# Causal weighted sums with key blocks at 0, 128, 256 and 384 instead of 0, 64, 192 and 320

## The chip, the cores and the metric

One Trainium2 chip, one of its cores. The metric is device time in microseconds (us), the median of several runs of the whole kernel; the profile is of one further execution.

## What is computed

Three layers follow each other on 4 batches of 448 positions: causal attention with 12 heads of 64, a gated feed-forward layer with a short convolution, and a layer of 4 experts, each a causal attention with a head of 64, of which each position takes the best two. Cut to what matters:

```python
def causal(q, k, v):                      # one head, 448 x 64
    scores = q @ k.T / 8, masked above the diagonal
    a = softmax(scores)
    return a @ v                          # the weighted sum

x   = causal(q, k, v)                     # 4 batches x 12 heads, fp32
h   = relu(x @ w_in)                      # 768 -> 1024
x   = (h * sigmoid(conv3(h))) @ w_out     # 1024 -> 768
out = sum over 2 of 4 experts of w_e * causal(x @ wq[e], x @ wk[e], x @ wv[e]) @ wo[e]
```

So there are 4 x 12 + 4 x 4 = 64 causal heads. The kernel takes them in pairs (`o` is 0 or 1 for the two heads): 24 pairs of the first layer and 8 of the experts, 32 in all.

## The kernel before

Queries stand in four blocks, `Q0` = 0, 64, 192, 320 with `QN` = 64, 128, 128, 128 rows; block `c` sees the first `Q0[c]+QN[c]` keys, that is 64, 192, 320 or 448. A pair passes these steps.

- **Scores** (`scores`, L619). For most pairs queries and keys are split in two parts each (`prepare`, L740), and three products per block are added; each head fills 64 of TensorE's 128 rows, and the two heads work side by side (L670). Pair 0 alone (`WHOLE_QK`, L40) skips the split: its keys are padded with zeros to 128 rows (`prepare_whole`, L757), and L661 multiplies whole fp32 numbers, one head after the other.
- **Weights.** VectorE masks and takes the maximum (L647), ScalarE the exponential (L651), and VectorE, ScalarE or GpSimd divide by the sum (L692, L695). They lie in a tile `e`, queries on the partitions.
- **Turning** (`weigh`, L706). TensorE turns 16 squares of 128x128 of `e` (`tr`, L704), so that keys lie on the partitions. In the first four squares the last 64 keys of head 0 lie beside the first 64 of head 1 (their keys are stored in opposite orders). Four copies take the turned squares from PSUM to SBUF, one of 448 columns (`n0`) and three of 512 (`ab`), on ScalarE (L606) or VectorE (L608).
- **The weighted sum.** The values of the pair lie in a tile `block`. L723 is one product over all 128 columns of TensorE, the first 64 keys of both heads, 448 queries. L729 holds six products of 64 columns each, for the key blocks at 64, 320 and 192 and both heads; here the two heads fill the left and the right half of the columns and work side by side. Each fp32 product is recorded as two instructions.

So TensorE works in three arrangements: the whole array (L704, L723, L877 and others), two halves of rows (L670), two halves of columns (L729).

All other matrix products are those of the feed-forward and projections (L877, L984). Two weight matrices are multiplied into one at the start (`fold`, L837).

No loop sets the order. Every step is entered in a `Plan` (L165) with its engines, an estimated cost and the buffers that it needs; a list scheduler then writes out the instructions of each engine in one fixed order, which the chip follows. A table of numbers (`SHIFTS`, L60) moves ranks in it. `FILLS` (L54) enters 30 products of zeros (L1079), which the plan places where TensorE has nothing else. All DMAs are issued in one queue, SP's.

Of the kernel before, what the change touches and what calls it, by code (L numbers as in the profile page):

```python
# [39 lines left out]
WHOLE_QK = range(1)  # L40


TILES = (((0, 1, 1), (0, 2, 1), (0, 3, 1), (0, 3, 3)), ((1, 1, 1), (1, 2, 1), (1, 3, 1), (1, 3, 3)), ((0, 2, 2), (0, 3, 2), (1, 2, 2), (1, 3, 2)))
SWITCH = 0.2
# [5 lines left out]
PAIRS, VALUES, UNITS, SLABS, EN, PO = 18, 6, 15, 3, 3, 1  # L50
QUOTA = {"xs": 7, "qks": 4, "y": 4, "vs": 3, "vs2": 2, "w1": 3, "wraw": 1, "ab": 4, "qw": 1, "kb": 1, "raw": 1}
# [34 lines left out]
def f32(ap):  # L86
    return ap.bitcast(F32)
# [73 lines left out]
class Op:  # L161
    __slots__ = ("n", "engines", "fn", "deps", "after", "bufs", "new", "rank", "wait", "ready", "start", "end", "engine", "m", "issue", "banks", "port")


class Plan:  # L165
# [25 lines left out]
    def op(self, engines, fn, r=(), w=(), after=(), hold=(), m=128, issue=0.45, port=""):  # L191
# [4 lines left out]
        o.m, o.issue = m, issue  # L196
# [145 lines left out]
    def schedule(self, rank):  # L342
# [20 lines left out]
        dge = dma = load = port = 0.0  # L363
        coming = {e: [] for e in names}
# [25 lines left out]
        while left:  # L390
# [19 lines left out]
            for e in names:  # L410
# [8 lines left out]
                while lists[e]:  # L419
# [9 lines left out]
                    if t > now + 1e-9:  # L429
                        heapq.heappush(events, t)  # L430
                    elif not o.new or room(o.new, now):
                        wait = max(now, load + o.m / 1200) - now if e == "T" else 0.0
                        found.append((item[0] + 500 * wait, len(found), item))
                        if wait <= 1e-9 or len(found) == 12:
                            break
# [19 lines left out]
                elif e == "T":  # L455

                    begin = max(now, load + o.m / 1200)
# [66 lines left out]
def attention_moe_moe(ctx: ExitStack, tc: tile.TileContext, qk, vv, w_in, cw, w_out, wqk, wvg, wo, out):  # L524
# [12 lines left out]
    mask = base.tile([128, 768], F32, name="mask")  # L537
# [3 lines left out]
                            base=0, pattern=[[-1, 128]], channel_multiplier=1)  # L541
    tri = base.tile([128, 4, 4], F32, name="tri")
# [21 lines left out]
    for t in blocks:  # L564
        for o in range(2):
            nc.gpsimd.memset(t[HALF[1 - o], 0, o], 0.0)
# [19 lines left out]
    for name, kind, quota in (  # L586
            ("xs", pairs, QUOTA["xs"]), ("g", pairs, 8), ("qks", pairs, QUOTA["qks"]), ("wx", pairs, 12),
            ("y", pairs, QUOTA["y"]), ("q2", pairs, 2), ("k2", pairs, 2),
            ("vs", bk, QUOTA["vs"]), ("gx", gxk, 1), ("vs2", bk, QUOTA["vs2"]), ("w1", slabs, QUOTA["w1"]), ("wraw", half, QUOTA["wraw"]), ("wt", half, 2), ("wxr", half, 2), ("raw", half, QUOTA["raw"]),
# [546 lines left out]
```

## Time and profile before

| | |
|---|---|
| Median of 3 runs | 540.93 us (540.92 to 541.36) |
| The profiled execution, its own time | 540.68 us |
| Its span in the profile, first to last instruction | 538.9 us |
| TensorE's granted clock over the span | 1.00, that is 2.4 GHz |
| Busy: PE, DVE, ACT, POOL | 530.6, 413.1, 331.7, 97.5 us |

PE is TensorE multiplying and PEld TensorE loading weights, DVE is VectorE, ACT ScalarE, POOL GpSimd. A matmul's length in the profile includes the time until its last result is out, so that lengths of neighbours overlap; what an instruction costs its successors is the distance from start to start.

### The profile page before, as it was taken

The numbers are of one execution on the slowest core, as the hardware profiler recorded it, in microseconds if no ns is written. First come the engines' busy times: TensorE is split into PE (matmuls) and PEld (weight loads), VectorE is DVE, ScalarE is ACT, GpSimd is POOL, SyncE is SP. The second block draws the span as 40 slices with busy tenths as digits, with TensorE's granted clock in tenths as the row PEclk, the third lists the DMA queues.
The fourth block names the chain that finished last, engine by engine and source line by source line (L and its number), as shares of the span: only waits on it lengthen the run. The fifth ranks groups of instructions, "written<-read, shape, count | busy, mean of one in ns | idle before, by whom it ended". The sixth has DMA issues, their size and how long they took to land.

```text
span 538.9 us, 10192 instructions
## 1 busy us (share of the span) xinstructions
PE 530.6 (98%) x3550; PEld 437.5 (81%) x3552; DVE 413.1 (77%) x1224; ACT 331.7 (62%) x947; POOL 97.5 (18%) x122
## 2 busy tenths in 40 slices
PE   8999999999999999999999999999999999999999
PEld 4768887678888887899887778998887778999886
DVE  5997869999995578794669988964877898855461
ACT  3973637668995456762557885752866668534442
POOL 3630102342343121200024210000232000000020
DMA  8785327656466002646002472671004405520042
GB/s 252 241 233 141 115 75 243 188 196 226 145 231 165 2 17 53 216 148 216 0 18 81 136 229 84 226 237 42 2 2 137 155 1 176 183 111 1 1 161 103
DMA packets 43411, 69.91 MB, mean 130 GB/s; under 512 B 8928, under 2 KB 37344, under 8 KB 43360
## 3 DMA queue, kind: packets, MB, share of 16 engines
q1 hardware_dynamic: 43360, 69.26, 40.7%
q8 instruction: 28, 0.46, 0.4%
q14 instruction: 23, 0.19, 0.1%
HBM read 55.87 MB, written 13.37 MB: 128 GB/s over the span
## 4 chain that ended last, share of the span: by engine, by line
PE 69%; DVE 3%; ACT 2%; DMA 1%; issue 0%; DVEq 0%; ACTq 0%
PE pf L877 41%; PE bank L704 8%; PE bank L670 7%; PE bank L729 6%; PE bank L723 4%; PE pf L984 1%; DVE work L906 1%; DMA work<-in_w_in 1%; PE bank L877 1%; ACT e L651 1%; PE pf L1079 1%; DVE work L914 0%; ACT e L692 0%; DVE work L798 0%; DVE work L800 0%; ACT pair L606 0%
## 5 line engine op out<-in xcount | busy, mean ns | idle before, releaser
L877 PE MATMUL pf<-pair,slab 128*128 128x448 f32 (+2 forms) x984 | 215.7, 367 | 1.6 <-DVE wqks L614 0.8
L877 PEld LDWEIGHTS pf<-pair,slab 128*128 128x128 f32 x984 | 171.8, 188 | 23.7 <-issue 6.1
L651 ACT ACTIVATE e<-e,stat 128x320 f32<-128x320 f32 (+3 forms) x256 | 126.8, 498 | 24.0 <-DVE stat L647 23.7
L647 DVE CUSTOM_DVE_ANT_0 e<-bank,mask 128x320 f32<-128x320 f32 (+3 forms) x256 | 92.7, 414 | 5.4 <-PE bank L670 4.9
L877 PE MATMUL pf<-pair,wqks 128*128 128x448 f32 x384 | 81.6, 369 | 0.5 <-ACT pair L606 0.5
L704 PE MATMUL bank<-ident,e 128*128 128x128 f32 x512 | 74.8, 276 | 2.7 <-DVE e L695 1.8
L877 PEld LDWEIGHTS pf<-pair,wqks 128*128 128x128 f32 x384 | 71.4, 188 | 7.1 <-ACT pair L606 0.9
L704 PEld LDWEIGHTS bank<-ident,e 128*128 128x128 f32 x512 | 59.3, 140 | 21.2 <-issue 7.6
L608 DVE COPY work<-bank 128x512 f32<-128x512 f32 (+1 forms) x63 | 40.6, 666 | 25.1 <-PE bank L704 22.1
L614 POOL TENSOR_TENSOR pair<-work,pair 128x448 fp32r<-128x448 f32 (+1 forms) x35 | 43.5, 1256 | 53.5 <-ACT pair L606 25.4
L606 ACT ACTIVATE work<-bank 128x512 f32<-128x512 f32 (+1 forms) x69 | 38.7, 579 | 22.9 <-PE bank L704 17.7
L670 PE MATMUL bank<-pair,pair 64*64 64x64 f32 (+3 forms) x560 | 51.8, 292 | 0.0
L906 DVE SCALAR_TENSOR_TENSOR work<-hp,cws,work 128x448 f32<-128x448 f32 x64 | 43.8, 696 | 7.0 <-ACT work L901 6.8
L729 PE MATMUL bank<-work,block 128*64 128x128 f32 (+2 forms) x384 | 48.5, 388 | 0.0
L651 ACT ACTIVATION_READ_ACCUMULATOR e<-e,stat 128x1 f32 (+1 forms) x256 | 48.3, 189 | 0.0
L670 PEld LDWEIGHTS bank<-pair,pair 64*128 64x128 f32 (+1 forms) x560 | 40.1, 173 | 3.6 <-issue 1.6
L729 PEld LDWEIGHTS bank<-work,block 128*64 128x64 f32 x384 | 22.5, 136 | 23.9 <-issue 21.1
L692 ACT ACTIVATE e<-e,stat 128x448 f32<-128x448 f32 (+3 forms) x88 | 39.0, 508 | 3.6 <-DVE stat L687 3.4
L877 PE MATMUL pf<-wvs,pair 128*128 128x260 f32 x288 | 37.7, 286 | 0.0
L614 DVE TENSOR_TENSOR pair<-pf,pair 128x448 fp32r<-128x448 f32 (+3 forms) x32 | 15.4, 500 | 28.7 <-ACT pair L606 28.4
L877 PEld LDWEIGHTS pf<-wvs,pair 128*128 128x128 f32 x288 | 35.3, 188 | 1.2 <-issue 0.6
L606 ACT ACTIVATE pair<-pf 128x448 fp32r<-128x448 f32 (+3 forms) x32 | 13.3, 443 | 37.0 <-PE pf L877 36.9
(98 smaller groups left out, 596.7 us busy)
## 6 DMA issues: line engine op xcount, KB each, us to landing
slab<-w_scratch SPq DMA_DIRECT2D x24, 768.0 KB, 4.3
work<-in_w_out SPq DMA_DIRECT2D x8, 768.0 KB, 5.1
work<-in_w_in SPq DMA_DIRECT2D x8, 768.0 KB, 5.6
w_scratch<-slab SPq DMA_DIRECT2D x8, 768.0 KB, 4.1
work<-in_qk SPq DMA_DIRECT2D x24, 224.0 KB, 4.0
out<-work SPq DMA_DIRECT2D x24, 224.0 KB, 2.0
block<-in_vv SPq DMA_DIRECT2D x24, 192.0 KB, 3.3
slab<-wo_scratch SPq DMA_DIRECT2D x6, 768.0 KB, 4.3
```

Of the source, the lines that this page charges most:

```text
L606: nc.scalar.activation(dst(), src(), AF.Copy)
L608: nc.vector.tensor_copy(dst(), src())
L614: return lambda e: engine(e).tensor_sub(dst(), src(), f32(h()))
L647: nc.vector.tensor_tensor_reduce(out=ec(o, c), in0=bank(o, c), in1=m, scale=-0.125, scalar=3.0e38, op0=OP.add, op1=OP.min, accum_out=st[ro ...
L651: nc.scalar.activation(ec(o, c), ec(o, c), AF.Exp, bias=st[rows, 0, o, c:c + 1], scale=-1.0, accum_out=st[rows, 1, o, c:c + 1])
L670: nc.tensor.matmul(bank(o, c), q(s)[own, Q0[c]:Q0[c] + QN[c]], k(t)[own, kc(o, c)], start=i == 0, stop=i == 2)
L692: nc.scalar.activation(ec(o, c), ec(o, c), AF.Copy, scale=st[:QN[c], 3, o, c:c + 1])
L704: P.op({"T": TURN}, lambda _: nc.tensor.transpose(dst(), src(), ident[:, :]), r=r, w=keys)
L723: P.op({"T": 4 * S / 2400}, lambda _: nc.tensor.matmul(ps[:, :S], v[:, 0].rearrange("p o d -> p (o d)"), n0[:, :S], start=True, stop=False ...
L729: nc.tensor.matmul(ps[own, Q0[k]:S], v[:, k, o], part(o), start=False, stop=k == 2)
L877: nc.tensor.matmul(out_ap(), a(), b(), start=first, stop=end), r=r, w=[(ps, 0)])
L906: return lambda _: nc.vector.scalar_tensor_tensor(cv[:, :S], hp[:, i:S + i], cws[:, fc, i:i + 1], cv[:, :S], op0=OP.mult, op1=OP.add)
```

## The change

Key blocks now begin at 0, 128, 256 and 384, so the blocks of keys have 448, 320, 192 and 64 columns of queries to serve (`KEYS`). All products of the weighted sum, the first included, have 64 columns per head and two heads side by side: eight in place of seven (L764). Half of the 128 keys of a block lie behind the first 64 queries that the block serves; that quarter of the triangle is not copied, its place holds zeros from the start.

The turned weights go to one buffer of their own, `z` (`ZN` = 1), in eight copies in place of four: four of 64 partitions x 128 columns, two of 128 x 512, two of 128 x 256. The products start when all eight are in. Before, `n0` and three `ab` were four separate buffers.

To suit, head 1's keys are now the ones stored backwards, in blocks of 64 (`keys`; 256-byte runs), the values of a pair come in four DMAs of 256-byte runs instead of three, the experts' values have one double tile instead of four quarters of a shared kind, and their copies are cut otherwise. `WHOLE_QK` covers pairs 0 and 1. The plan counts 0.094 us for each change of TensorE's arrangement and puts an operation that needs one behind others (`CHANGE`, `TURNING`). `SHIFTS` is another table.

```diff
-WHOLE_QK = range(1)
+WHOLE_QK = range(2)
+KEYS = ((0, 448), (448, 320), (768, 192), (960, 64))
+def spread(z, width, first, step, n):
+    lo = min(first, width - 2 * step)
+    return z[:, lo:lo + 2 * step].rearrange("p (b c) -> p b c", b=2)[:, :, first - lo:first - lo + n]
+CHANGE, TURNING = 0.094, 2.0
...
-                        found.append((item[0] + 500 * wait, len(found), item))
+                        other = e == "T" and o.mode != mode
+                        found.append((item[0] + 500 * wait + TURNING * other, len(found), item))
...
     def weigh(e, v, v_r, dst):
-        ps, n0 = P.buf("po"), P.buf("ab")
-        t = P.buf("ta")
+        ps, z, t = P.buf("po"), P.buf("z"), P.buf("ta")
...
-        P.op(psum_cost(S, "AV"), high(lambda: n0[:, :S], lambda t=t: t[:, :S]), r=[(t, c) for c in range(4)], w=[(n0, 0)])
+        for o, own in enumerate(HALF):
+            for i, (first, step, src, near) in enumerate(((0, 448, 64, 128), (768, 192, 320, 128))):
+                P.op(psum_cost(128, "AV"), high(lambda own=own, n=1024 * o + first, step=step: spread(z, 2048, n, step, 64)[own],
+                                                lambda own=own, t=t, src=src: spread(t, 512, src, near, 64)[own]),
+                     r=[(t, c) for c in range(4)], w=[(z, (o, i))])
...
-        P.op({"T": 4 * S / 2400}, lambda _: nc.tensor.matmul(ps[:, :S], v[:, 0].rearrange("p o d -> p (o d)"), n0[:, :S], start=True, stop=False),
-             r=[(n0, 0)] + v_r, w=[(ps, 0)])
...
         def rest(_):
-            for k, part in ((1, lambda o: ab[o][:, :384]), (3, lambda o: ab[o][:, 384:]), (2, lambda o: ab[2][:, 256 * o:256 * o + 256])):
+            for k, (n0, n) in enumerate(KEYS):
                 for o, own in enumerate(HALF):
-                    nc.tensor.matmul(ps[own, Q0[k]:S], v[:, k, o], part(o), start=False, stop=k == 2)
+                    nc.tensor.matmul(ps[own, S - n:S], v(k, o), z[:, 1024 * o + n0:1024 * o + n0 + n], start=k == 0, stop=k == 3)
...
+    def keys(p, o, dst, w):
+        if o:
+            P.op(dma_cost(114688, 256), load(lambda: blocks64(dst()), blocks64(qk[p, HALF[1], 1])[:, ::-1]), w=w)
+        else:
+            P.op(dma_cost(114688, 1792), load(dst, qk[p, HALF[0], 1]), w=w)
```

The order of instructions that the plan writes out moves with it. The first place is TensorE's queue at the last weighted sum of the program, before (`work` holds the turned weights, `block` the values, `pair` and `slab` are operands of the last projection):

```order
L877 MATMUL bank_151<-pair_121,slab_142 128x448
L877 MATMUL pf_144<-pair_121,slab_142 128x448
L723 MATMUL bank_149<-work_143,block_100 128x448
L729 MATMUL bank_149<-work_143,block_100 64x384 x2
L729 MATMUL bank_149<-work_143,block_100 64x128 x2
L729 MATMUL bank_149<-work_143,block_100 64x256 x2
L877 MATMUL pf_144<-pair_121,slab_141 128x448
```

and of the change:

```order
L916 MATMUL bank_155<-pair_131,slab_151 128x448
L916 MATMUL bank_158<-pair_131,slab_151 128x448
L764 MATMUL bank_160<-z_113,values_110 64x448 x2
L764 MATMUL bank_160<-z_113,values_110 64x320 x2
L764 MATMUL bank_160<-z_113,values_110 64x192 x2
L764 MATMUL bank_160<-z_113,values_110 64x64 x2
L916 MATMUL pf_154<-pair_131,slab_150 128x448
```

The product over the whole array is gone, and four pairs of products stand where there were three. In the same queue over the whole program the arrangement changes 118 times before and 107 times after.

The second place is ScalarE's queue around the copies of the last two weighted sums, before (`bank` is PSUM):

```order
L606 ACTIVATE work_143<-bank_149 128x448
L606 ACTIVATE pair_121<-bank_148 128x448
L606 ACTIVATE work_143<-bank_147 128x512
L606 ACTIVATE work_143<-bank_146 128x512
L606 ACTIVATE pair_124<-bank_149 128x448
```

and of the change:

```order
L633 ACTIVATE z_113<-bank_156 64x2x64 x4
L633 ACTIVATE z_113<-bank_155 128x2x256
L633 ACTIVATE z_113<-bank_157 128x2x128 x2
L633 ACTIVATE pair_145<-bank_160 128x448
```

The copies of one weighted sum are seven rows here (the eighth is on VectorE). In the whole program 128 copies become 256, of which ScalarE has 132 and VectorE 124.

The third place is TensorE's queue near the start, before, where four of the products of zeros (`mask` holds them) stand between whole scores and the first folded weights:

```order
L661 MATMUL bank_149<-work_143 64x64
L1079 LDWEIGHTS mask
L1079 MATMUL pf_144<-mask 128x512
L1079 LDWEIGHTS mask
L1079 MATMUL pf_145<-mask 128x512
L661 MATMUL bank_150<-work_143 64x64
L1079 LDWEIGHTS mask
L1079 MATMUL pf_144<-mask 128x512
L1079 LDWEIGHTS mask
L1079 MATMUL pf_145<-mask 128x512
L877 MATMUL pf_144<-pair_121,slab_140 128x512
```

and of the change, where 19 of them stand ahead of the first row:

```order
L1110 LDWEIGHTS mask
L1110 MATMUL pf_153<-mask 128x512
L688 MATMUL bank_155<-work_152 128x448
L688 MATMUL bank_156<-work_152 128x448
L688 MATMUL bank_157<-work_152 128x320
L688 MATMUL bank_158<-work_152 128x320
L731 MATMUL bank_159<-ident,work_152 128x128
```

Of the 30 products of zeros, 12 stood ahead of the first real product before and 19 do now; 11 stood behind the last real product of the program, and none does now.

## Rows read from the trace of the kernel before

**Rows 1.** The page, parts 1 and 4: busy time; the chain by engine.

```profile
PE 530.6 (98%) x3550; PEld 437.5 (81%) x3552; DVE 413.1 (77%) x1224; ACT 331.7 (62%) x947; POOL 97.5 (18%) x122
...
PE 69%; DVE 3%; ACT 2%; DMA 1%; issue 0%; DVEq 0%; ACTq 0%
```

**Rows 2.** Waits of PE: us in total, times, longest us.

```profile
PE bank L704 <- DVE e L695: 1.8, 2, 1.1
PE pf L585 <- DVE tri L543: 1.7, 1, 1.7
```

**Rows 3.** Stretches: length, busy us (instructions) of PE, PEld, DVE, ACT, POOL; clock.

```profile
0.00:40.00 40.00, 35.91 (x213) 24.68 (x214) 33.33 (x104) 26.29 (x75) 18.04 (x37) 1.00 0.83 243
...
81.00:150.00 69.00, 67.03 (x469) 52.35 (x465) 67.03 (x165) 54.87 (x150) 23.13 (x18) 1.00 0.64 202
...
320.00:500.00 180.00, 180.00 (x1193) 151.47 (x1191) 137.29 (x421) 108.83 (x313) 15.07 (x22) 1.00 0.32 103
```

**Rows 4.** Groups of PE instructions by shape.

```profile
L723 PE MATMUL bank<-work,block 128*128 128x448 f32 x64 | 30.0, 550 | 0.0
L729 PE MATMUL bank<-work,block 128*64 128x384 f32 x128 | 27.7, 512 | 0.0
...
L729 PE MATMUL bank<-work,block 128*64 128x256 f32 x128 | 19.2, 379 | 0.0
...
L729 PE MATMUL bank<-work,block 128*64 128x128 f32 x128 | 12.4, 273 | 0.0
```

**Rows 5.** Timeline of PE, 300 to 312 us: start, length, instruction.

```profile
301.57 0.91 PE L723 MATMUL bank<-work,block 128*128 128x448 f32 x2
302.41 0.24 PE L670 MATMUL bank<-pair 64*64 64x64 f32 x2
...
304.16 1.52 PE L729 MATMUL bank<-work,block 128*64 128x384 f32 x12
305.61 0.66 PE L704 MATMUL bank<-ident,e 128*128 128x128 f32 x4
...
309.05 0.92 PE L723 MATMUL bank<-work,block 128*128 128x448 f32 x2
```

**Rows 6.** Timeline of PE near the end.

```profile
520.98 0.92 PE L723 MATMUL bank<-work,block 128*128 128x448 f32 x2
521.73 0.82 PE L704 MATMUL bank<-ident,e 128*128 128x128 f32 x6
...
535.20 2.55 PE L1079 MATMUL pf<-mask 128*128 128x512 bf16 x10
```

**Rows 7.** Timeline of PEld, from 304.15 to 304.23 us.

```profile
304.16 0.20 PEld L729 LDWEIGHTS bank<-work,block 128*64 128x64 f32 x4 [0.19 <-issue]
```

**Rows 8.** Timeline of PE at the start.

```profile
5.94 2.75 PE L1079 MATMUL pf<-mask 128*128 128x512 bf16 x12
8.76 0.74 PE L704 MATMUL bank<-ident,work 128*128 128x128 f32 x5
```

**Rows 9.** Groups of ACT copies by shape.

```profile
L606 ACT ACTIVATE work<-bank 128x512 f32<-128x512 f32 x48 | 27.8, 594 | 7.5 <-PE bank L704 6.4 <-PE bank L723 0.5 <-issue 0.2
...
L606 ACT ACTIVATE work<-bank 128x448 f32<-128x448 f32 x21 | 11.3, 543 | 15.4 <-PE bank L704 11.4 <-PE bank L877 1.8 <-DMA out<-work 1.4
...
L606 ACT ACTIVATE block<-pf 128x128 f32<-128x128 f32 x11 | 2.7, 280 | 6.4 <-PE pf L877 6.4
...
L606 ACT ACTIVATE slab<-bank 128x256 fp32r<-128x256 f32 x4 | 1.5, 378 | 0.4 <-PE bank L704 0.4
```

**Rows 10.** DMA issues: KB each, us to landing.

```profile
block<-in_vv SPq DMA_DIRECT2D x24, 192.0 KB, 3.3
...
block<-in_vv SPq DMA_DIRECT2D x48, 16.0 KB, 2.9
```

**Rows 11.** Page, part 5: weight loads of L729.

```profile
L729 PEld LDWEIGHTS bank<-work,block 128*64 128x64 f32 x384 | 22.5, 136 | 23.9 <-issue 21.1
```

**Rows 12.** 81 to 150 us, L729 alone: length, PE, PEld.

```profile
81.00:150.00 69.00, 9.09 (x72) 4.22 (x72) 1.00 0.64 202
```

More of the change, by code (lines that the diff above doesn't have):

```diff
@@ L161 @@
 class Op:
-    __slots__ = ("n", "engines", "fn", "deps", "after", "bufs", "new", "rank", "wait", "ready", "start", "end", "engine", "m", "issue", "banks", "port")
+    __slots__ = ("n", "engines", "fn", "deps", "after", "bufs", "new", "rank", "wait", "ready", "start", "end", "engine", "m", "issue", "banks", "port", "mode")
 class Plan:
@@ L565, in attention_moe_moe @@
         for o in range(2):
-            nc.gpsimd.memset(t[HALF[1 - o], 0, o], 0.0)
+            nc.gpsimd.memset(t[HALF[1 - o], 3, o], 0.0)
+    both_values = tiles("values", 1, [128, 4, 2, 2, 64], F32)
+    for t in both_values:
+        for o in range(2):
+            nc.gpsimd.memset(t[HALF[1 - o], 3, :, o], 0.0)
+    turned_weights = tiles("z", ZN, [128, 2048], F32)
+    for t in turned_weights:
+        for o in range(2):
+            for n0, n in KEYS:
+                nc.gpsimd.memset(t[HALF[1 - o], o * 1024 + n0:o * 1024 + n0 + 64], 0.0)
     weights = tiles("e", EN, [128, 2048], F32)
@@ L645, in mx @@
             def mx(_):
-                m = mask[rows, 448 - w:448] if c and o else mask[rows, 320:320 + w]
+                m = mask[rows, 384:384 + w] if c and o else mask[rows, 448 - w:448] if c else mask[rows, 320:384]
                 nc.vector.tensor_tensor_reduce(out=ec(o, c), in0=bank(o, c), in1=m, scale=-0.125, scalar=3.0e38,
@@ L670, in mm @@
                             nc.tensor.matmul(bank(o, c), q(s)[own, Q0[c]:Q0[c] + QN[c]], k(t)[own, kc(o, c)], start=i == 0, stop=i == 2)
-            P.op({"T": 0.27 + sum(3 * max(product(Q0[c] + QN[c]), QN[c] / 1200) for c in ORDER)}, mm, r=r,
-                 w=[(sbs[o][c], c) for c in ORDER for o in range(2)], hold=[e])
+            P.op({"T": 0.08 + sum(3 * max(product(Q0[c] + QN[c]), QN[c] / 1200) for c in ORDER)}, mm, r=r,
+                 w=[(sbs[o][c], c) for c in ORDER for o in range(2)], hold=[e], mode=1)
             for c in ORDER:
@@ L933, in load_cw, with halves @@
         single(lambda: raw[:, :6 * NF], 3 * NF, lambda: bits(cws).rearrange("p a b -> p (a b)"), [(raw, 0)], [(CWS, 0)])
-    def turn(step, o, dst, src, *more):
-        parts = [(lambda ap: ap, lambda ap: ap)] if o else turned
-        steps = [step(lambda d=d: d(dst()), lambda q=q: q(src()), *[lambda d=d, m=m: d(m()) for m in more]) for d, q in parts]
-        def fn(e):
-            for f in steps:
-                f(e)
-        return fn
+    def halves(step, o, own, ap, *more):
+        d = blocks64 if o else lambda ap: ap
+        q = (lambda ap: blocks64(ap)[:, ::-1]) if o else d
+        return step(lambda: d(ap()), *[lambda m=m, f=f: f(m()) for m, f in zip(more, (q, d))])
     def project(b, gs, gx):
@@ L1003, in project @@
-            P.op(cost[1], high(lambda n=n, c=c: lg[:n, b, c], lambda src=src: src()[:, 256:260]), r=[key], w=[(LG, (b, c))])
+                P.op(psum_cost(128, "AV"), high(lambda k=k: v[:, k, :, 0], lambda ps=ps: heads(ps, 0)), r=[(ps, 0)], w=[(v, (k, 0))])
+                for i in range(2):
+                    P.op(psum_cost(128, "AV"), high(lambda k=k, i=i: v[HALF[i], k, :, 1], lambda ps=ps, i=i: heads(ps, 1)[HALF[1 - i]]), r=[(ps, 0)], w=[(v, (k, 1 + i))])
+                for i in range(2):
+                    dst = (HALF[1 - i] if k or i else own), k + i
+                    P.op(psum_cost(4), high(lambda dst=dst: lg[dst[0], b, dst[1]], lambda ps=ps, i=i: ps[HALF[i], 256:260]), r=[(ps, 0)], w=[(LG, (b, dst[1], i))])
@@ new lines, in project @@
+                continue
+            for f in range(NF):
+                for m, s in ((128, 0), (64, 1))[::1 if f + 1 < NF else -1]:
+                    P.op({"T": product(260)}, lambda _, f=f, m=m, s=s, ps=ps: nc.tensor.matmul(
+                        ps[:m, :260], gx[:, f * 128:f * 128 + m], wvs[:, s, f], start=f == 0 and s == 0, stop=f + 1 == NF and s == 0),
+                         r=[(gx, f), (WV, (f, s))], w=[(ps, 0)], m=m)
+            xc = P.buf("xc")
+            P.op(psum_cost(260), high(lambda xc=xc: xc[own, :260], lambda ps=ps: ps[oth, :260]), r=[(ps, 0)], w=[(xc, 0)])
@@ new lines, in project @@
+            P.op({"V": on_vector(260)}, lambda _, ps=ps, xc=xc: nc.vector.tensor_add(xc[own, :260], ps[own, :260], xc[own, :260]),
+                 r=[(ps, 0)], w=[(xc, 0)])
+            for o in range(2):
+                P.op(copy_cost(128, "AV"), high(lambda o=o: v[HALF[o], 3, :, o], lambda xc=xc, o=o: heads(xc, o)[own]), r=[(xc, 0)], w=[(v, (3, o))])
+            P.op(copy_cost(4, "AVG"), high(lambda: lg[oth, b, 3], lambda xc=xc: xc[own, 256:260]), r=[(xc, 0)], w=[(LG, (b, 3, 0))])
+        vs = [(lambda k, o, a=a: v[:, k, a, o], [(v, (k, i)) for k in range(4) for i in range(3 if k < 3 else 2)]) for a in range(2)]
```

123 lines of the change are left out of this document (53 added, 70 removed), and 24 rows, old and new, of the table SHIFTS.

## The prediction

> **What bounds the kernel now.** I read the busy times first, then the chain that ended last, then TensorE's waits, then stretches of the span, and at last the instructions one by one. PE is busy for 530.6 of 538.9 us, and the chain runs through PE for 69% of the span where DVE has 3% and ACT 2% [rows 1]. The longest wait of PE by one cause adds up to 1.8 us, the next is the 1.7 us before the very first instruction [rows 2]. From 320 to 500 us PE has no idle time at all, with DVE at 137 and ACT at 109 of 180 us; only in the first 40 us does it stand idle for some 4 us [rows 3]. So the sum of what TensorE does sets the end, and an instruction that it no longer executes is gained in full, as long as the plan keeps finding it other work. The one stretch where another engine is as full is 81 to 150 us: DVE 67.0 and ACT 54.9 of 69 us [rows 3].
>
> **The change, part by part.**
>
> *The products.* One weighted sum costs now: L723, 0.75 us from its start to that of a transpose behind it [rows 6], and L729, 1.45 us from 304.16 to 305.61 [rows 5]. When L723 is followed by products in halves of rows instead of a transpose the distance is 0.84 us [rows 5], so a change of arrangement costs 0.09 us, and L729 without the change behind it 1.36. Together 2.11 us. What a column costs comes from the groups by shape: the 128 groups of 256 columns take 19.2 us and those of 128 take 12.4, that is 6.8 us for 32 sums x 128 columns, 1.66 ns per column of queries and pair of heads, four passes included [rows 4]. At this price 448 columns cost 0.74 us, what L723 costs too: the same time for a block with half the rows in use, or rather for two heads with 64 keys each. Afterwards the pair of heads has 448+320+192+64 = 1024 columns in halves where L729 had 768: 1.36 + 256 x 1.66 ns = 1.79 us. The gain is 2.11 - 1.79 = 0.32 us, for 32 sums -10.4 us. The uncertain part is the 64-column products, which the trace does not hold in this form: if loading their weights bounds them they cost what 128 columns cost, 0.11 us more, and the gain is 7.0 us. Four weight loads of L729 lie within 0.20 us [rows 7] and one takes 0.136 us on average [rows 11], so all four began within some 0.06 us of each other: the loads of the two halves overlap. I take -10.4, bounds -7.0 and -10.4.
>
> The Trainium skill, page "TensorE: Matmul & The Clock Gate", section "LDWEIGHTS (loading the stationary operand)", gives a load the number of its columns divided by 1.2 in ns; from that page, an estimate, four loads of 64 columns one after another take 0.21 us, as much as the products of 128 columns, and by it the sum would be 3.4 us smaller. The trace does not agree that the four stand one after another, and the same skill, page "TensorEngine Tiling (Array Packing)", section "Key Properties", lets separate tiles load in parallel.
>
> *Changes of arrangement.* The order has 107 instead of 118. 11 x 0.09 = -1.0 us; between -1.0 and 0, should the dearer ones be those that stay.
>
> *Pair 1 whole.* Its scores take 2 x 1024 columns at 1.66 ns, 3.40 us, in place of one L670 group, 1.75 us from 302.41 to 304.16 [rows 5]: +1.7. Nothing is split for this pair, which takes a copy and two subtractions off ACT, DVE and POOL in the first 40 us. If PE would have waited there anyway, the cost is 0. I take +1.7.
>
> *Products of zeros.* Twelve take 2.75 us, 0.23 each [rows 8]. Before, 11 of 30 stand behind the last product, at 535.20 [rows 6], where they delay nothing; afterwards all 30 stand ahead of it: +2.5 us. They stand where the plan finds nothing else to do, so they may take the place of the idle time in the first 40 us; then the cost is 0. PE's first real work, now at 8.76 us [rows 8], comes seven such products later, 1.6 us. I take +2.5, as an instruction in the queue is executed whether data came early or not.
>
> *The copies.* Before, one copy of 448 columns and three of 512, on ACT 0.54 + 3 x 0.59 = 2.33 us; afterwards four of 128 (nearest row 0.28, of twice the partitions), two of 512 and two of 256 (0.38): 1.12 + 1.19 + 0.76 = 3.07 us [rows 9]. That is +0.74 us per sum, 24 us over the run, spread over ACT and DVE, which are idle for 207 and 126 us. The cover is that idle time, and it is missing from 81 to 150 us: L729 has 72 instructions there, six sums [rows 12], 4.4 us more work for a DVE with 2 us left and an ACT with 14 [rows 3]. Between 0 and +4.4; since ACT has room for all of it and the plan decides who copies, I take +1.0.
>
> *Loads.* Each pair keeps seven DMAs (four for q and k, three for the values become three and four), but the values come in 256-byte runs. Such a DMA of 16 KB lands after 2.9 us, 192 KB in long runs after 3.3 [rows 10]. If the first pair's four landed one after the other that would be 11.6 in place of 6.2, once, +5.4 us; later ones are fetched ahead, and no DMA is among PE's long waits [rows 2]. SP's queue has ten DMAs of values ahead of the second w_out tile now (none before), which the fold needs next. Between 0 and +5.4, I take 0, because those 11.6 us run beside scores and exponentials of the pair. The other copies (experts' values, keys) change by a few instructions of 0.3 us on ACT and DVE and go with the copies above.
>
> Sum: -10.4 - 1.0 + 1.7 + 2.5 + 1.0 = -6.2. The profiled execution took 540.68 us: 534.5. The median of the runs is 0.25 above that execution, so 534.7 us.
>
> **The rivals.**
>
> *The single buffer makes TensorE wait (slower).* All copies of the next sum must wait until the last product of this one has read `z`; before, `n0` was free after the first product and its successor could be filled. Two sums follow at 7.5 us (301.57 and 309.05, [rows 5]). The buffer is taken for 3.07 us of copies if one engine does them, 1.79 of products, and for four transposes between (L704, 6 in 0.82 us, [rows 6]) some 0.5: 5.4 us. That leaves 2.1 us for the handovers and for waiting behind exponentials in ACT's queue. Once the copies wait longer than that, TensorE runs out of prepared work; from 0.26 us lost in each of the some 24 sums in dense stretches the gain is gone. At 0.4 us: +9.6 - 6.2, 544.1 us. Against it: ACT stood idle for 7.5 and 15.4 us before such copies until PE was done [rows 9], so it is the copies that wait for PE today. The skill's tiling page, section "PSUM Bottleneck", says that tiling speeds up TensorE but not the emptying of PSUM, which speaks for this rival.
>
> *The 64-column products cost as much as 128 columns* (their loads in a row): -7.0 for -10.4, 538.1 us.
>
> *The head costs nothing:* zeros and whole scores replace idle time; -10.4 - 1.0 + 1.0, 530.3 us, 530.5 as median. For it: 4 us of idle in the first 40. Against it: the zeros and whole scores stand in PE's queue, and what follows them, limited by PE too, does not start earlier for the idle time that they replace.
>
> *Nothing remains:* the products at -7.0 and the copies at their full 4.4 us in the full stretch: -7.0 - 1.0 + 1.7 + 2.5 + 4.4 = +0.6, 541.5 us.
>
> **How the numbers follow.** My forecast has a chance of 0.56 (its own range 532 to 537.5), the wait for the buffer 0.13, dear small products 0.12, a free head 0.13, nothing remains 0.06. A difference under 0.2%, 1.1 us, can hardly be told from none here. Faster are the forecast, the small products and the free head: 0.81; the same 0.06; slower 0.13. The range from 529.8 to 540.6 holds the forecast, the dear products and the free head, and leaves out the wait and nearly all of the last.
>
> **What would show it.** The step of L764 between its 320- and 192-column groups must again be 1.66 ns per column, and all its instructions some 57 us from start to start; if the group of 64 columns is as long as one of 128 would be, the second rival holds. PE's busy time should fall by the same 6 us as the span. If waits of L731 or L764 for ACT or DVE add up to more than some 5 us, the buffer or the copies are the cause; if the first real product starts at 10 us and the last folded weight no later than before, the head was free. The prediction is wrong if PE's idle time grows by more than the products shrink.

## The result, and the profile after

| | before | after |
|---|---|---|
| Median, runs taken together | 541.07 us (540.92 to 541.36) | 534.35 us (534.15 to 534.56) |
| Span of the profiled execution | 538.9 us | 532.6 us |
| Ratio, 95% interval | | 0.9875 (0.9858 to 0.9892) |

The kernel is 6.7 us faster; the forecast was 6.2 faster, 534.7 us. The page of the profile of after, the lines that answer to [rows 1]:

```profile
PE 523.3 (98%) x3606; PEld 439.7 (83%) x3608; DVE 412.1 (77%) x1275; ACT 343.3 (64%) x1017; POOL 94.4 (18%) x136
PE 93%; DVE 3%; DMA 2%; issue 1%; ACT 0%; SPq 0%; ACTq 0%
```

PE's busy time fell by 7.3 us, ACT's rose by 11.6, and the chain that ended last now runs through PE for 93% of the span (69% before). TensorE is still the bound. Its longest waits of after, beside [rows 2] (line, what it waited for, us in total, times, longest):

```profile
PE pf L612 <- DVE tri L561: 1.8, 1, 1.8
PE bank L731 <- DVE work L839: 1.3, 1, 1.3
PE bank L731 <- DVE e L722: 0.9, 3, 0.4
PE bank L688 <- DMA work<-in_qk: 0.7, 1, 0.7
PE bank L731 <- DVE z L635: 0.5, 1, 0.5
```

The new buffer `z` appears once, with 0.5 us. The stretches of after, beside [rows 3]:

```profile
0.00:40.00 40.00, 35.12 (x190) 22.39 (x192) 29.84 (x91) 21.98 (x60) 14.04 (x39) 1.00 0.78 210
81.00:150.00 69.00, 68.35 (x497) 56.02 (x497) 66.65 (x182) 61.73 (x180) 29.80 (x31) 1.00 0.66 208
320.00:500.00 180.00, 180.00 (x1239) 155.60 (x1238) 133.91 (x419) 106.55 (x315) 18.62 (x26) 1.00 0.33 103
```

From 81 to 150 us ACT took 7 us more and DVE none, and PE was busy for 1.3 us more than before. In the first 40 us PE idles as long as before, a little longer even. So the copies found room, and the head did not become better. From 150 to 320 us the idle time went from 0.9 us to nearly nothing, before and after:

```profile
150.00:320.00 170.00, 169.10 (x1169) 142.52 (x1169) 127.07 (x409) 107.40 (x321) 34.07 (x40) 1.00 0.36 115
150.00:320.00 170.00, 169.97 (x1227) 146.10 (x1226) 132.72 (x437) 116.76 (x358) 27.93 (x35) 1.00 0.40 117
```

The products by shape (one group each, count, busy us, mean ns), for the pairs of the first layer, which have the tile `block`:

```profile
L764 PE MATMUL bank<-z,block 128*64 128x448 f32 x96 | 23.6, 565 | 0.0
L764 PE MATMUL bank<-z,block 128*64 128x320 f32 x96 | 17.2, 432 | 0.0
L764 PE MATMUL bank<-z,block 128*64 128x192 f32 x96 | 12.1, 326 | 0.0
L764 PE MATMUL bank<-z,block 128*64 128x64 f32 x96 | 7.1, 220 | 0.0
```

From 320 to 192 columns the step is 5.1 us for 24 sums x 128 columns, 1.66 ns per column; from 192 to 64 it is 5.0 us, 1.63 ns. The smallest products lie on the same line, so the loading of weights does not bound them down to 64 columns. One whole weighted sum, in TensorE's timeline of after:

```profile
301.50 1.95 PE L764 MATMUL bank<-z,block 128*64 128x448 f32 x16
303.38 1.53 PE L731 MATMUL bank<-ident,e 128*128 128x128 f32 x12
```

It takes 1.88 us to the start of the transposes behind it, or 1.79 without the 0.09 of the change of arrangement, as forecast.

The head is another matter. TensorE's and then VectorE's rows of after:

```profile
6.02 4.45 PE L1110 MATMUL pf<-mask 128*128 128x512 bf16 x19
10.31 2.74 PE L688 MATMUL bank<-work 128*128 128x448 f32 x8
```

```profile
8.67 0.96 DVE L641 TENSOR_TENSOR pair<-work,pair 128x772 fp32r<-128x772 f32 x1 [6.57 <-ACT pair L633]
9.67 0.56 DVE L835 TENSOR_SCALAR work<-work 128x768 int32<-128x768 int32 x1
```

The first real product starts at 10.31 instead of 8.76 us [rows 8]. The conversion of the first tile of `w_out`, L835, starts at 9.67 us; in the trace of before the same instruction starts at 6.06. SP's queue of after, where its second tile follows at 13.13 us (before: 8.75):

```profile
5.38 6.54 SPq L644 DMA_DIRECT2D block<-in_vv x10
12.04 0.52 SPq L644 DMA_DIRECT2D work<-in_wqk x1
12.61 0.43 SPq L644 DMA_DIRECT2D work<-in_wvg x1
13.13 0.38 SPq L644 DMA_DIRECT2D work<-in_w_out x1
```

What comes later for it are the fold's products, which need the converted tiles. In the first 40 us TensorE of before did 72 instructions of its line L877, 14.75 us; after did 37 of L916:

```profile
0.00:40.00 40.00, 8.22 (x37) 6.12 (x38) 1.00 0.78 210
```

The last folded weights are written 8.7 us later, at 107.2 us instead of 98.5 (before and after: count, shortest, median and longest ns, first and last start in us):

```profile
L614 DVE TENSOR_TENSOR wvs<-pf,wvs x8: 408/419/428, 33.2 to 98.5; 128x260 fp32r<-128x260 f32 x8
L641 DVE TENSOR_TENSOR wvs<-pf,wvs x8: 375/420/429, 38.6 to 107.2; 128x260 fp32r<-128x260 f32 x8
```

The last product of the program ends at 529.12 us, with the row below; in the kernel before it ended at 535.35 us, as the last products of zeros began [rows 6].

```profile
525.65 3.47 PE L916 MATMUL bank<-pair,slab 128*128 128x448 f32 x16
```

TensorE's time up to the start of the last product can be divided by what it did: the distance from each instruction's start to the next one's, idle time apart, added up over either trace (us).

| | before | after | change |
|---|---|---|---|
| Weighted sums (L723, L729; L764) | 69.7 | 60.5 | -9.2 |
| Transposes, fold and projections, warm-up | 396.0 | 395.6 | -0.4 |
| Scores, whole and split | 58.3 | 61.1 | +2.8 |
| Products of zeros | 3.8 | 5.7 | +1.9 |
| Idle | 7.1 | 5.8 | -1.3 |
| Sum | 535.0 | 528.8 | -6.2 |

The cost of a change of arrangement lies in whichever row stands ahead of it. In the first 40 us zeros and idle time together grew by some 2.6 us; behind 40 us idle time fell by 2.1, which no term of the prediction named.

### The profile page after: what moved, and what is told of

Its sections match the earlier page's. It is cut to its first block, busy times and chain, and to the rows that moved or that the text cites. A ratio compares the mean times of both kernels' runs of the same rounds, so it can differ in the third digit from the quotient of the medians.

```text
span 532.6 us, 10424 instructions
## 1 busy us (share of the span) xinstructions
PE 523.3 (98%) x3606; PEld 439.7 (83%) x3608; DVE 412.1 (77%) x1275; ACT 343.3 (64%) x1017; POOL 94.4 (18%) x136
## 4 chain that ended last, share of the span: by engine, by line
PE 93%; DVE 3%; DMA 2%; issue 1%; ACT 0%; SPq 0%; ACTq 0%
PE pf L916 56%; PE bank L731 11%; PE bank L764 11%; PE bank L697 9%; PE bank L688 2%; PE pf L1024 1%; DMA work<-in_qk 1%; PE pf L1110 1%; PE bank L916 1%; PE pf L612 1%; DVE e L674 1%; DVE pair L641 1%; DVE e L722 1%; DMA block<-in_vv 0%; SPq L644 0%
## 5 line engine op out<-in xcount | busy, mean ns | idle before, releaser
L916 PE MATMUL pf<-pair,slab 128*128 128x448 f32 (+2 forms) x984 | 216.7, 367 | 0.2 <-ACT work L633 0.2
L916 PEld LDWEIGHTS pf<-pair,slab 128*128 128x128 f32 x984 | 170.7, 188 | 18.7 <-issue 1.4
L678 ACT ACTIVATE e<-e,stat 128x192 f32<-128x192 f32 (+3 forms) x256 | 127.1, 499 | 24.7 <-DVE stat L674 24.2
L674 DVE CUSTOM_DVE_ANT_0 e<-bank,mask 128x192 f32<-128x192 f32 (+3 forms) x256 | 92.8, 413 | 10.6 <-PE bank L697 9.4
L916 PE MATMUL pf<-pair,wqks 128*128 128x448 f32 x384 | 81.8, 369 | 0.0
L731 PE MATMUL bank<-ident,e 128*128 128x128 f32 x512 | 77.1, 275 | 1.6 <-DVE e L722 0.9
L916 PEld LDWEIGHTS pf<-pair,wqks 128*128 128x128 f32 x384 | 71.1, 188 | 6.3 <-issue 0.6
L635 DVE COPY z<-bank 64x128 f32<-64x128 f32 (+2 forms) x124 | 47.7, 404 | 19.9 <-PE bank L731 17.6
L633 ACT ACTIVATE z<-bank 64x128 f32<-64x128 f32 (+2 forms) x132 | 46.5, 386 | 22.9 <-PE bank L731 13.4
L641 POOL TENSOR_TENSOR pair<-work,pair 128x448 fp32r<-128x448 f32 (+1 forms) x29 | 36.8, 1278 | 122.6 <-ACT pair L633 60.1
L764 PE MATMUL bank<-z,block 128*64 128x448 f32 (+3 forms) x384 | 47.1, 386 | 0.0
L764 PEld LDWEIGHTS bank<-z,block 128*64 128x64 f32 x384 | 25.9, 136 | 22.8 <-issue 13.3
L719 ACT ACTIVATE e<-e,stat 128x192 f32<-128x192 f32 (+3 forms) x82 | 36.8, 509 | 10.2 <-DVE stat L714 10.2
L641 DVE TENSOR_TENSOR pair<-work,pair 128x448 fp32r<-128x448 f32 (+1 forms) x53 | 34.5, 659 | 6.8 <-ACT pair L633 6.6
L916 PE MATMUL pf<-wvs,pair 128*128 128x260 f32 x288 | 38.9, 288 | 0.0
L916 PEld LDWEIGHTS pf<-wvs,pair 128*128 128x128 f32 x288 | 35.8, 189 | 0.8 <-issue 0.4
L641 DVE TENSOR_TENSOR pair<-pf,pair 64x448 fp32r<-64x448 f32 (+1 forms) x24 | 14.9, 621 | 25.5 <-ACT pair L633 25.4
```

The source lines that it names most:

```text
L633: nc.scalar.activation(dst(), src(), AF.Copy)
L635: nc.vector.tensor_copy(dst(), src())
L641: return lambda e: engine(e).tensor_sub(dst(), src(), f32(h()))
L674: nc.vector.tensor_tensor_reduce(out=ec(o, c), in0=bank(o, c), in1=m, scale=-0.125, scalar=3.0e38, op0=OP.add, op1=OP.min, accum_out=st[ro ...
L678: nc.scalar.activation(ec(o, c), ec(o, c), AF.Exp, bias=st[rows, 0, o, c:c + 1], scale=-1.0, accum_out=st[rows, 1, o, c:c + 1])
L719: nc.scalar.activation(ec(o, c), ec(o, c), AF.Copy, scale=st[:QN[c], 3, o, c:c + 1])
```

## The experiments

All are variants of the changed kernel unless the text says otherwise. The first seven keep its order of instructions, except for what is named; the others let the plan make a new order.

### The old products in the new order (e1_old_products)

```diff
-            for k, (n0, n) in enumerate(KEYS):
+            nc.tensor.matmul(ps[:, :S], v(0, 2), z[:, :S], start=True, stop=False)
+            for k, n0, n in ((1, 448, 384), (3, 960, 128), (2, 832, 256)):
```

One product over the whole array and six halves, with the old numbers of columns, at the same place in every queue; copies, loads and head are those of the change.

> The changed kernel with its order of instructions kept, but each weighted sum multiplied in the shapes of before: one product of 448 columns over the whole array, then pairs of 384, 128 and 256 columns in halves (the output is not the reference's). Copies, buffers, loads and the place of every other instruction stay. Theory, that the sum of TensorE's work sets the end: one weighted sum goes from 1.79 to 2.11 us, 32 x 0.32 = +10.3 us, and one more change of arrangement where the sum follows other products in halves, 11 x 0.09 = +1.0: +10 to +11.5 us over the changed kernel, about 545 us. Rival, that the gain came from the new order and the own buffer while the shapes lie beside other waits: less than +5 us.

Measured: 545.38 us (545.17 to 545.59), ratio to before 1.0077 (1.0063 to 1.0091). Undoing the products costs 545.38 - 534.35 = 11.0 us, within the +10 to +11.5 that the theory gave. In TensorE's queue the arrangement changes 118 times here, as before the change, and 107 times in the changed kernel, so the 11.0 stand for two terms of the prediction, -10.4 and -1.0. It says a second thing: with old products all the rest of the change costs 545.38 - 541.25 (before, run beside it) = 4.1 us, and the other terms of the prediction sum to 1.7 + 2.5 + 1.0 = +5.2.

### No products of zeros (e2_no_zeros)

```diff
-P.op({"T": 0.21}, lambda _, fill=fill: nc.tensor.matmul(fill[:, :], zeros[:, :128], zeros[:, :512], start=True, stop=True), w=[(fill, 0)])
+P.op({"T": 0.21}, lambda _: None, w=[(fill, 0)])
```

> The changed kernel without its 30 products of zeros behind the warm-up; nothing else moves. The prediction's price, that each such product costs TensorE its 0.22 us: 27 stand ahead of the last stretch, -5.9 us, or at least the -2.5 of the sum. Rival, that they stand in for waits that the same data would cause anyway: between -1 and +0.5 us, and the idle time of PE in the first 17 us grows by what they took.

Measured: 535.32 us (533.8 to 535.68), ratio 0.9886 (0.987 to 0.9903): no gain; by the median it is 1 us slower than after, outside the rival's -1 to +0.5 but far from the theory's -2.5 and less. The five executions spread from 533.8 to 535.68 us, and the profiled one took 533.8, less than any of after, so its trace can't show what the median lost. TensorE's timeline shows why the head gains nothing:

```profile
9.74 5.31 PE L688 MATMUL bank<-work 128*128 128x448 f32 x8 [4.29 <-DMA work<-in_qk]
```

and the stretch from 10 to 14 us (the granted clock, 0.50, stands behind the five engines' busy times) shows that the products behind the wait are slow:

```profile
10.00:14.00 4.00, 4.00 (x7) 1.97 (x7) 3.97 (x7) 0.43 (x1) 0.00 (x0) 0.50 0.48 112
```

Without zeros TensorE stands idle for 4.3 us until q and k have landed, begins only 0.6 us earlier, and then runs at half clock, 1.2 GHz: the same eight products last 5.31 us instead of 2.74. The Trainium skill, page "TensorE: Matmul & The Clock Gate", section "Part 1: The HAM clock gate (the "warmup" mystery)", calls the slow clock the default, which activity releases; the trace agrees, with 0.50 from 10 to 14 us and 1.00 again from 18 us on.

The rest of the head makes up for both. The changed kernel waits at 22 us for q and k of the next pair, this one does not, and at 32 us both wait for the same converted tile (to 32.32 us in after, 32.44 here). Near the end the two traces are level, without zeros and then after:

```profile
515.96 1.95 PE L764 MATMUL bank<-z,values 128*64 128x448 f32 x16
516.02 1.95 PE L764 MATMUL bank<-z,values 128*64 128x448 f32 x16
```

So the products of zeros in the head cost nothing. Two that stand behind this row in after cost 0.6 us (the next weighted sum starts at 520.16 and 520.79 us); the kernel before had two in that place as well.

### Small copies twice (e3_double_copies)

```diff
+    def twice(f):
+        return lambda e: (f(e), f(e))
...
-                P.op(psum_cost(128, "AV"), high(lambda own=own, n=1024 * o + first, step=step: spread(z, 2048, n, step, 64)[own],
-                                                lambda own=own, t=t, src=src: spread(t, 512, src, near, 64)[own]),
+                P.op(psum_cost(128, "AV"), twice(high(lambda own=own, n=1024 * o + first, step=step: spread(z, 2048, n, step, 64)[own],
+                                                      lambda own=own, t=t, src=src: spread(t, 512, src, near, 64)[own])),
```

Each of the four copies of 64x128 of a weighted sum is executed twice on its engine.

> The changed kernel with each of the 128 small copies (64 partitions x 128 columns) made twice: 53 x 0.27 us more on ACT and 75 x 0.29 on DVE, 36 us of added work, one sum's copies 1.1 us longer. Theory, that the copies lie beside TensorE's work and only the full stretch shows them: 0 to +5 us. Rival, the single buffer: if copies stand on the path between one sum's products and the next one's, 0.5 us or more for most of the 32 sums, +15 us and above, with PE waiting on ACT and DVE from 150 us on.

Measured: 555.23 us, ratio 1.026 (1.0246 to 1.0275), 20.9 us slower than after. 128 more copies are 75 of 286 ns on DVE and 53 of 267 on ACT, 36 us of work, so more than half of it reached the end. The theory (0 to 5 us) missed, and the rival's bound of 15 was passed. PE's longest waits:

```profile
PE bank L734 <- DVE z L635: 4.0, 4, 1.5
PE bank L734 <- DVE stat L677: 2.5, 5, 1.0
PE bank L734 <- ACT z L633: 2.3, 3, 1.0
PE bank L700 <- DVE z L635: 2.1, 4, 1.0
```

It is in the stretch with the most room that the idle time appears: 8.3 of 180 us from 320 to 500, where after has none. So the idle time of ACT and DVE in such a table is not free for work that the order did not plan for. The waits for copies into `z` add up to some 10 us, most of them of transposes (L734) and scores (L700), which write to PSUM, and 1.3 us of the weighted sums themselves; others are for `stat`, which VectorE makes in the same fixed queue. How much of it the single buffer causes, as the rival had it, and how much the fixed queues was not separated.

### The first values later in SP's queue (e4_values_later)

```diff
+        for part, behind in ((late[:4], dma[25]), (late[4:], dma[31])):
+            for o in part:
+                order.remove(o)
+            i = order.index(behind) + 1
+            order[i:i] = part
```

The first twelve DMAs of values stand behind the loads of weights, q and k that followed them.

> The changed kernel with the first 12 DMAs of values moved back in SP's queue: the first pair's four stand behind the second pair's q and k, the next eight behind the third weight tiles; all other queues keep their order. In the changed kernel ten of them take 6.5 us of the queue from 5.4 us on, and 22.4 us of useful TensorE work is done by 40 us where 25.8 was before. Theory, that these issues delay the next weights and keys and that the later stages have no slack to make it up: 1 to 3 us faster than the changed kernel, with the waits of PE for q and k at 22 us and for the converted tile at 31 us gone. Rival, that the head is held by the order on DVE and by fixed queue places on PE: within 0.5 us.

Measured: 538.65 us (537.23 to 540.62), ratio 0.9954 (0.9937 to 0.997): 4.3 us slower than after, so this theory fell in its sum. Its first half came true: the wait for q and k at 22 us is gone, and TensorE starts the first weighted sum at 27.61 us instead of 29.09. The wait for the converted tile stayed (1.45 us, at 31 us). SP had not been waiting on the values alone. It stood before the second `w_out` tile until VectorE had converted the first (L839 ends at 12.97 us), and the values filled that time. The second `w_out` is issued at 13.01 us here, 13.13 in after. The eight values that were moved farthest now delay the loads of the third pair:

```profile
25.75 5.45 SPq L653 DMA_DIRECT2D block<-in_vv x8
31.24 0.60 SPq L653 DMA_DIRECT2D work<-in_wvg x1
31.93 1.75 SPq L653 DMA_DIRECT2D work<-in_qk x3
```

(26.97 and 27.97 us in after). TensorE then waits (1.5 us for the third load of weights, up to 35.1 us), and the granted clock falls with it; the second weighted sum starts at 66.4 us instead of 61.7:

```profile
34.00:40.00 6.00, 4.58 (x24) 3.44 (x26) 4.58 (x9) 3.41 (x8) 2.25 (x2) 0.74 0.66 173
40.00:50.00 10.00, 10.00 (x64) 8.69 (x60) 5.83 (x21) 3.94 (x14) 2.27 (x2) 0.82 0.79 182
```

### The price of a change of arrangement (e5_half_between, e5_whole_between)

```diff
+                if k < 3:
+                    nc.tensor.matmul(ps[HALF[0], :64], zeros[:, :64], zeros[:, :64], start=False, stop=False)
```

and, for the second kernel, `ps[:, :64]` and `zeros[:, :128]`.

> The changed kernel in its own order, with a tiny product of zeros (64 columns of weights, 64 columns of zeros, one half of TensorE's columns) after each of the first three pairs of products of a weighted sum: 96 more products, no change of arrangement. It is the control of the next run. Both theories: 1 to 6 us slower than the changed kernel, 536 to 540 us.

> The same, but the 96 products of zeros take 128 columns of weights and so the whole array: 192 more changes of arrangement. Theory (each change costs 0.09 us of TensorE's time, as the prediction took from one place of the trace): 192 x 0.094 = 18 us slower than the control, 15 to 21. Rival (a change costs nothing of its own, what the one place showed was something else): within 4 us of the control.

Measured: 538.53 us (538.23 to 539.16) and 558.36 (557.63 to 559.03); ratios 0.9952 (0.994 to 0.9963) and 1.0313 (1.0299 to 1.0326). The difference is 19.8 us, 0.103 for each of 192 changes. The added products themselves, by shape, in the control and in the other kernel:

```profile
L766 PE MATMUL bank<-mask 128*64 128x64 bf16 x96 | 18.5, 193 | 0.0
```

```profile
L766 PE MATMUL bank<-mask 128*128 128x64 bf16 x96 | 19.5, 203 | 0.0
```

They last 193 and 203 ns, so only 1 us of the difference is in their own length; the rest is between neighbours. The loads of 128 columns for 64 are part of the 0.103, so the change itself costs at most that by this run. The Trainium skill, page "TensorEngine Tiling (Array Packing)", section "Key Properties", says that a change of mode drains the engine; it gives no time, and the trace gives 0.09 to 0.10 us.

### w_out first in the head (e6_w_out_first)

```diff
+        vec, dma = ([o for o in order if o.engine == e] for e in "VD")
+        for o, ahead in [(vec[i], vec[0]) for i in (1, 3, 4)] + [(dma[20], dma[12])]:
+            order.remove(o)
+            order.insert(order.index(ahead), o)
```

> The changed kernel with its head put in another order and nothing else: VectorE converts the first tile of w_out (three instructions) ahead of the subtraction that waits for ScalarE's copy, and SP issues the second tile of w_out ahead of the values of pairs 1 and 2. Theory (the head is bound by the chain of w_out tiles through VectorE and SP, and the changed kernel left VectorE idle until 8.7 us while the tile had landed): the later waits of TensorE for the conversion (1.3 us at 32 us) and for q and k (0.7 us at 22 us) shrink, 0.5 to 2 us faster than the changed kernel, 532.3 to 533.9 us. Rival (the subtraction that is put off feeds TensorE's next operand, so TensorE then waits there): equal or slower, 534 to 536 us, with a new wait of TensorE for the pair's tile near 16 us.

Measured: 539.45 us (536.91 to 539.79), ratio 0.9956 (0.994 to 0.9973), 5 us slower than after. The profiled execution took 536.91 us, so its trace accounts for 2.5 us of the 5; what the median lost beside is not shown. VectorE's row of the moved conversion:

```profile
8.62 0.56 DVE L841 TENSOR_SCALAR work<-work 128x768 int32<-128x768 int32 x1 [6.52 <-ACT pair L639]
```

The conversion writes to the tile from which ScalarE's copy and VectorE's subtraction read, so it could not begin before ScalarE's copy (8.62 us); and as it now stands ahead of the subtraction, the operand of that subtraction is overwritten and the low part comes out wrong. So the changed kernel starts the conversion 3.6 us later than the old one, and 2.6 of these (8.62 for 6.06) are the tile's, not the queue's. POOL shows the price of the other half of the edit, a load of weights that now comes behind the second `w_out`, for which SP stands until 11.20 us:

```profile
19.19 0.83 POOL L643 TENSOR_SCALAR pair<-work 128x772 fp32r<-128x772 f32 x1 [3.58 <-DMA work<-in_wvg]
```

(15.84 us in after, without a wait), and TensorE stands for it:

```profile
20.08 3.73 PE L922 MATMUL pf<-pair,slab 128*128 128x512 f32 x11 [1.59 <-POOL pair L643]
```

### Without the tables of shifts (r1_new_plain_order, r2_old_plain_order)

```diff
-SHIFTS = (
-...
-)
+SHIFTS = ()
```

in the changed kernel and in the kernel before.

> The changed kernel, with its table of shifts emptied, so that the plan stands as the scheduler first makes it. Theory (the products of the weighted sums are the gain, whatever the order): the shifts of either kernel only tune the order, so this kernel stays 7 to 12 us ahead of the old kernel without its own shifts, at a level that may lie 2 to 15 us above the tuned ones; its instructions of the weighted sums are again 57 us from start to start. Rival (the gain lies in the new table of shifts): the two kernels without shifts are within 3 us of each other.

> The kernel before, with its table of shifts emptied. Theory: 7 to 12 us slower than the changed kernel with an empty table. Rival (the table is the gain): within 3 us of it.

Measured: 546.15 us (545.59 to 548.75) for the new kernel and 543.94 (543.89 to 544.12) for the old one; ratios 1.01 (1.0074 to 1.0126) and 1.0051 (1.0034 to 1.0067). Both expectations missed: the difference is small as the rival said, but with the other sign. The first lines of their pages, new and then old:

```profile
PE 525.9 (97%) x3606; PEld 440.2 (81%) x3608; DVE 412.0 (76%) x1256; ACT 341.8 (63%) x1022; POOL 112.3 (21%) x149
```

```profile
PE 531.4 (98%) x3549; PEld 439.3 (81%) x3552; DVE 406.2 (75%) x1222; ACT 331.6 (61%) x947; POOL 103.5 (19%) x125
```

TensorE is busy for 5.5 us less in the new kernel here too. But it idles for 543.9 - 525.9 = 18.0 us, the old one for 542.1 - 531.4 = 10.7. The first 40 us hold 7.8 us of the idle time (5.9 in the old), and the waits are many and short:

```profile
PE pf L901 <- DVE pair L626: 2.7, 3, 1.8
PE bank L716 <- DVE e L707: 2.4, 1, 2.4
PE pf L901 <- ACT pair L618: 1.7, 1, 1.7
PE bank L716 <- DVE stat L659: 1.3, 2, 1.0
```

So TensorE has less work with the tables and without them, but without them the time does not fall: the new table is worth 546.15 - 534.35 = 11.8 us to the new kernel, the old one 543.94 - 541.25 = 2.7 us to the old.

### Pair 1 split, without the table (r3_new_plain_one_whole)

```diff
-WHOLE_QK = range(2)
+WHOLE_QK = range(1)
```

> The changed kernel with an empty table, and with pair 0 alone multiplied whole, as before the change; pair 1 is split. The prediction's term for pair 1 is +1.7 us of products, so by it this kernel is 1 to 2.5 us faster than the changed one with an empty table. Rival (the whole scores of pair 1 stand where TensorE would wait for data or for the split): equal within 1 us, or slower, with more waits of TensorE for VectorE, ScalarE or GpSimd in the first 40 us. A plan that is made anew moves by 1 to 2 us by itself, so only a larger difference decides by the time; else the waits in the first 40 us decide.

Measured: 551.78 us (549.98 to 553.63), ratio 1.0195 (1.016 to 1.0229): 5.6 us slower than r1, no gain of 1.7. In its head TensorE waits for q and k, and the clock falls to half for the stretch behind:

```profile
18.00:22.00 4.00, 0.83 (x7) 0.51 (x5) 0.00 (x0) 0.25 (x1) 0.00 (x0) 0.86 0.89 289
22.00:26.00 4.00, 3.50 (x7) 2.27 (x8) 2.47 (x4) 2.21 (x4) 0.00 (x0) 0.50 0.46 120
```

The longest wait, 3.7 us, is for q and k of pair 0, which is whole in either kernel. The plan made another order, so the 5.6 us are not the price of splitting a pair, and this run does not decide about the +1.7.

### Two buffers z, without the table (e7_two_z_fewer_pairs, e7_two_z_two_e)

```diff
-PAIRS, VALUES, UNITS, SLABS, EN, PO, ZN = 18, 4, 11, 3, 3, 1, 1
+PAIRS, VALUES, UNITS, SLABS, EN, PO, ZN = 16, 4, 10, 3, 3, 1, 2
```

and, in the second kernel, `18, 4, 11, 3, 2, 1, 2`.

> The changed kernel with an empty table of shifts and two buffers z; the room for the second is taken from the tiles of pairs (16 for 18) and of units (10 for 11). With one buffer the changed kernel with an empty table takes 546.2 us, though its TensorE has less to do than the old one's. Theory (the single buffer is what keeps the plan from filling TensorE's queue, the price that the prediction's first rival named): 538 to 543 us, with TensorE idle for 5 us less or more. Rival (the single buffer is not what costs the untuned order; the plan just makes another order): 544 us or above.

> The same with the room for the second z taken from the tiles e of the weights (2 for 3), all other tiles as they were. Theory (single buffer): 538 to 544 us. Rival: 544 us or above; one tile e less may cost something of its own, so a slow result here decides little without the other run.

Measured: 554.55 us (551.86 to 556.12) and 542.2 (541.4 to 543.1); ratios 1.0244 (1.0202 to 1.0286) and 1.0021 (1.0011 to 1.003). With a second `z` for one `e` the new kernel without a table is 4 us faster than r1, as the theory said; with one paid for by tiles of pairs and units it is 8.4 us slower, against it. Four nearly equal programs without a table lie between 542 and 555 us, so a difference of 4 us between two of them is within what a new order moves anyway. Whether the single buffer costs the untuned order something stays open. In the tuned order it does not, beyond 0.5 us of waits.

## Why the prediction was right

The size was right within 0.4 us, and the main mechanism was the one forecast: TensorE's work sets the end, and the weighted sums became cheaper. That the sum came out so close was luck in part. The table behind the result has errors of 1 to 2 us in single terms, and they cancel.

- **TensorE's work sets the end.** Right: PE has no idle time from 320 to 500 us in either kernel, and 0.03 us from 150 to 320 in after. The clause "as long as the plan keeps finding it other work" was passed over too lightly. Without the tables the same saving of PE's work is lost in idle time (r1, r2). A chance for that belonged among the rivals.
- **Products -10.4 and arrangement -1.0.** Right in kind: the slope, the 1.79 us of a sum and the 64-column products are as forecast. The size of the two together, -11.4, is -11.0 by e1. Between the two traces it is -9.6 (weighted sums -9.2, transposes and projections -0.4). Why the old products cost more in the new order than in their own is not shown. The price of a change is right, 0.09 to 0.10 us (e5). PE's busy time fell by 7.3 us, the span by 6.3.
- **Pair 1 whole +1.7.** Too low: the scores take 2.8 us more between the traces. From start to start the one whole pair takes 3.9 us before (L661) and the two take 8.2 after (L688), where the prediction had 3.40 for a pair.
- **Zeros +2.5.** Wrong as reasoned. "An instruction in the queue is executed whether data came early or not" is true, but here data came late: q and k landed at 9.7 us, when the 19 zeros were nearly done (e2). Zeros did move ahead of the last product (+1.9 us between the traces), into a head that waits for the converted tile at 32 us with them and without. Leaving them out gains nothing there and drops the clock for a stretch.
- **Loads 0.** The step named what would be late, the second `w_out` tile behind ten values, and then priced it at nothing. It is late by 4.4 us, though not for the values: it waits for VectorE's conversion, whose tile ScalarE's copy must first have read (e4, e6). The fold's products come later for it. The values cost something too: with them moved back the first weighted sum starts 1.5 us earlier (e4), though other loads then come late. The head does cost something, as the forecast said against the rival of a free head: zeros and idle time grew by some 2.6 us there. That the loads and conversions cost it, and not the zeros, follows from the waits; both attempts to move them (e4, e6) ended slower.
- **Copies +1.0.** The one wait for a copy into `z` in the trace is 0.5 us, so 0 to 0.5 as far as waits show. The reason, room on ACT, holds for copies that were planned for (81 to 150 us) and not for others (e3).
- **The rest as a sum.** e1 puts all but products and arrangement at +4.1 us; pair 1, zeros and copies were +5.2. Between the traces scores, zeros and idle time make 2.8 + 1.9 - 1.3 = +3.4. The prediction has no term for the idle time behind 40 us, which fell by 2.1; by that luck the head's cost and the smaller gain of the products did not show in the sum. What of the new order or its table brought those 2.1 us is not shown.
- **The rivals.** The wait for the single buffer did not come in this order. The dear 64-column products are refuted by the step of 1.63 ns and by the 1.79 us of a whole sum. Of the free head one half holds: the first real product starts at 10.3 us and the zeros are free, but the last folded weights come 8.7 us later, and the head as a whole is not free.

By the medians no variant was faster than the changed kernel.

## What to carry to other kernels

When one engine is busy for 98% of the span, count its instructions by start-to-start distances: such a count gave 11.4 us here, changes of arrangement included, where undoing the products measured 11.0. But a fixed order must be made anew for the new work, as here 11.8 us hung on it against a saving of the same size. Where single terms can be checked in two traces, check them: a right sum can hide errors that cancel. And before pricing filler work in a head, look for when the first operands land: up to there filler cost nothing here, and without it the clock fell.

## What the runs showed of the hardware that was not expected

After 4.3 us without work TensorE had half its clock, 0.50 from 10 to 14 us in e2, and in r3 the same from 22 to 26 us after a wait of 3.7 us; the eight products at the start of e2 took 5.31 instead of 2.74 us. So such a stall is followed by slow products, at 1.2 GHz. In the profiled execution of e2 the end did not show it, as the head waits for data later on; in e4 a clock of 0.74 and 0.82 from 34 to 50 us is part of a delay that lasts to the end. In the changed kernel itself the clock stays at 1.00 in every stretch up to 500 us.

A tiny product of 64 columns between the halves of a weighted sum costs 538.53 - 534.35 = 4.2 us for 96, 0.044 us each, though each is recorded with 193 ns; in the other arrangement the same product costs 0.25 us.
